# Attention into a GEGLU block: batch 0's row sums in four groups of rows, with a rewritten start

## The chip, the cores and the metric

The kernel runs on one core of one Trainium2 chip. The metric is device time in microseconds, given as the median of a few executions; the profile is of one of those executions. All times in the text that are "at" a moment count from the start of the profiled span.

## The reference

Eight batches of sliding-window attention (8 heads, 576 tokens, 64 per head, window 128, ALiBi bias) feed a gated block of 512 by 1536.

```python
scores = scale * np.matmul(q, k.transpose(0, 1, 3, 2))
mask = (rel >= 0) & (rel < window)
scores = np.where(mask, scores + bias[None], -1000000000.0)
attn = np.exp(scores - np.max(scores, axis=-1, keepdims=True))
attn = attn / (np.sum(attn, axis=-1, keepdims=True) + 1e-09)
attn_out = np.matmul(attn, v)
# ... heads side by side: x has 4608 rows (tokens) of 512
g = x @ w_gate
out = (0.5 * g * (1.0 + erf(g / sqrt(2)))) * (x @ w_val) @ w_out
```

## The kernel before

PE (the matrix engine) does everything in the order in which it is written: transposes, scores, row sums, products with the values, gate and value products, output products. Heads go in four pairs, `c`. A batch is cut into part one (320 tokens) and part two (256). Sums of the exponentials are products with a stationary operand of ones, one column group of PE for each pair, with a column for every token; DVE takes the reciprocal, and four f32 products spread it over the 64 rows of each head:

```python
def sums(b, s):
    ps = bank()
    for j, a, e in PIECES[s]:
        for i in (0, 1):
            for c in range(4):
                nc.tensor.matmul(
                    out=ps[32 * c:32 * c + 32, a:e],
                    lhsT=ones[:, min(j, 1), i, :], rhs=prob(b, s, c, i, j, e - a), ...)
    ...
    lo, hi = PART[s]
    nc.vector.reciprocal(sumrow[b][:, lo:hi], ps[:, 0:hi - lo])     # 128 x 320, then 128 x 256

def spread_pe(b, s, copies=(nc.scalar.copy, nc.vector.tensor_copy)):
    lo, hi = PART[s]
    pss = [bank() for _ in range(4)]
    for c, ps in enumerate(pss):
        nc.tensor.matmul(out=ps[:, 0:hi - lo], lhsT=sel[32 * c:32 * c + 32, ...],
                         rhs=sumrow[b][32 * c:32 * c + 32, lo:hi], ...)
    for c, ps in enumerate(pss):
        copies[c % 2](out=recip[b][:, c, lo:hi], in_=ps[:, 0:hi - lo])
```

Products of zeros stand in front of some steps. They compute nothing; each is 512 columns wide. `keep_busy(n)` puts `n` of them before the next bank that is used:

```python
def bank():
    ps = psum.tile([128, 512], FP32, name="ps")
    for _ in range(heat.pop()):
        nc.tensor.matmul(out=ps, lhsT=zeros[:, 0:128], rhs=zeros, start=True, stop=True)
    heat.append(0)
    return ps
```

The order of batch 0, which is all that the change touches, is:

```python
keep_busy(8); first((0, 1))                 # transposes of tokens 0-383; keep_busy(1) before the keys'
keep_busy(1)
scores(0, 0, (0, 1), lambda: (keep_busy(1), first((2,)), first((3,))))
scores(0, 0, (2, 3))
scores2(0)
keep_busy(2); rest((0, 1)); rest((2, 3))    # transposes of tokens 384-575
keep_busy(4); sums(0, 0)
keep_busy(2); scores(0, 1, (0, 1), None, masks)
keep_busy(3); spread_pe(0, 0)
values(0, 0, range(4))
scores(0, 1, (2, 3), None, masks)
for f in range(4): gate_val(0, f, 0, 320, tails)
...
sums(0, 1)
...
for f in (4, 5): gate_val(0, f, 0, 320)
spread_pe(0, 1)
values(0, 1, range(4))
gate_val(0, 6, 0, 320)
```

The softmax here doesn't subtract the row's maximum and nothing guards it: scores larger than these inputs give would overflow.

## Time and profile before

| what | before |
|---|---|
| time, median of 3 (range) | 359.17 us (358.96 to 359.27) |
| profiled span | 357.6 us |
| PE busy | 97% |
| keys of the first transfer landed | 7.03 us |
| first reciprocal | 15.29 to 17.45 us |
| first gate product on the value side | 21.11 us |
| first transposes of batch 1 | 40.66 us |
| end of the last copy on ACT | 354.99 us |

### The profile page before, as it was taken

Reading aid. Unit: us, or ns where it says so; the run is one execution under the profiler, and the core shown is the slowest. Engines: PE = TensorE matmul, PEld = TensorE weight load, DVE = VectorE, ACT = ScalarE, POOL = GpSimd, SP = SyncE. Lnnn points to the kernel's source line nnn. Section 1 sums busy time; section 2 is a strip of 40 time slices with the busy share of each in tenths; the row PEclk is TensorE's granted clock in tenths of the full one; section 3 lists DMA queues with packets and bytes.
Section 4 is the critical chain, followed back from the end, with each engine's and each line's share of the span. In section 5 each row is a group of like instructions: output and inputs, shape, how many; then the busy total and the mean of one; then the engine's idle time right before and its main releaser. Section 6 shows DMA issues by size and latency. Waiting matters only on the chain.

```text
span 357.6 us, 6808 instructions
## 1 busy us (share of the span) xinstructions
PE 346.0 (97%) x2703; PEld 172.8 (48%) x2746; DVE 188.9 (53%) x309; ACT 185.5 (52%) x342; POOL 105.8 (30%) x141
## 2 busy tenths in 40 slices
PE   7799999999999999999999999999999999999996
PEld 2468545444455445445454545445454444444444
DVE  4877568443888746656446554746473503302420
ACT  4874496535878367532973288336833123313322
POOL 8954579501920085002920094004000000000000
PEclk9999999999999999999999999999999999999999
DMA  9999999999999299683997599969206030011002
GB/s 104 176 193 195 200 148 181 164 179 137 151 140 140 49 188 179 120 173 68 142 199 147 110 103 211 154 132 71 86 33 132 4 116 0 3 59 59 2 20 97
DMA packets 146144, 42.61 MB, mean 119 GB/s; under 512 B 133144, under 2 KB 139032, under 8 KB 146112
## 3 DMA queue, kind: packets, MB, share of 16 engines
q0 software_dynamic: 106880, 18.88, 69.3%
q1 hardware_dynamic: 36432, 17.31, 21.7%
q10 hardware_dynamic: 2800, 5.99, 7.8%
q8 instruction: 21, 0.34, 0.4%
q14 instruction: 11, 0.09, 0.1%
HBM read 43.65 MB, written 9.53 MB: 149 GB/s over the span
## 4 chain that ended last, share of the span: by engine, by line
PE 87%; DVE 5%; ACT 4%; issue 2%; DMA 1%; POOL 0%; DVEq 0%; ACTq 0%; POOLq 0%
PE ps L310 49%; PE ps L333 24%; PE ps L291 4%; PE ps L179 4%; DVE r L254 3%; ACT P L186 2%; PE ps L245 2%; DMA ks<-in_k_dram 1%; PE ps L274 1%; DVE kT L150 1%; PE ps L140 1%; PE ps L347 1%; PE ps L70 0%; DVE hT L317 0%; DVE xT L297 0%
## 5 line engine op out<-in xcount | busy, mean ns | idle before, releaser
L317 DVE TENSOR_TENSOR hT<-ps,gelu 128x512 bf16<-128x512 f32 (+2 forms) x115 | 74.0, 653 | 106.1 <-PE ps L310 91.7
L316 ACT ACTIVATE gelu<-ps 128x512 bf16<-128x512 f32 (+2 forms) x115 | 65.2, 571 | 116.9 <-PE ps L310 112.3
L310 PE MATMUL ps<-xT,wv 128*128 128x512 bf16 (+2 forms) x453 | 111.4, 366 | 0.6
L310 PE MATMUL ps<-xT,wg 128*128 128x512 bf16 (+2 forms) x444 | 110.9, 366 | 1.0
L333 PE MATMUL ps<-wo,hT 128*128 128x512 bf16 x402 | 94.9, 380 | 0.8
L186 ACT ACTIVATE P<-ps 128x512 bf16<-128x512 f32 x144 | 73.4, 625 | 8.1 <-PE ps L179 8.1
L310 PEld LDWEIGHTS <-wv 128*128 128x128 bf16 x460 | 44.7, 98 | 49.1 <-issue 0.3
L310 PEld LDWEIGHTS <-wg 128*128 128x128 bf16 x460 | 43.2, 98 | 47.4 <-issue 0.6
L189 DVE TENSOR_TENSOR P<-P,emask 128x1024 bf16<-128x1024 bf16 x72 | 48.2, 691 | 32.0 <-ACT P L186 31.9
L333 PEld LDWEIGHTS <-hT 128*128 128x128 bf16 x420 | 38.8, 98 | 47.9 <-issue 4.0
L96 POOL DMA_DIRECT2D vb<-in_v_dram x40 | 34.0, 905 | 6.4 <-DMA ks<-in_k_dram 1.6
L338 ACT COPY osb<-ps 128x512 f32<-128x512 f32 x31 | 18.6, 601 | 29.6 <-PE ps L333 28.7
L254 DVE RECIPROCAL r<-ps 128x320 f32<-128x320 f32 (+1 forms) x16 | 30.7, 1937 | 2.9 <-PE ps L245 2.9
L525 POOL COPY mark<-hT 1x2 bf16<-1x2 bf16 x4 | 0.7, 175 | 100.3 <-DVE hT L317 100.3
L297 DVE TENSOR_TENSOR xT<-ps,rb 128x320 bf16<-128x320 f32 (+1 forms) x64 | 24.6, 445 | 7.3 <-DMA rb<-rd 5.3
L96 POOL DMA_DIRECT2D qs<-in_q_dram x30 | 25.2, 864 | 7.5 <-PE ps L179 2.9
L96 POOL DMA_DIRECT2D ks<-in_k_dram x30 | 25.4, 899 | 1.0 <-DMA qs<-in_q_dram 0.9
L179 PE MATMUL ps<-qT,kT 64*128 64x256 bf16 (+1 forms) x384 | 21.8, 244 | 2.3 <-DVE kT L150 1.8
L179 PEld LDWEIGHTS <-kT 64*128 64x128 bf16 x384 | 13.0, 94 | 14.3 <-issue 9.1
L291 PE MATMUL ps<-P,vb 128*64 128x128 bf16 (+2 forms) x384 | 18.2, 243 | 0.1
L291 PEld LDWEIGHTS <-vb 128*64 128x64 bf16 x384 | 14.7, 110 | 5.8 <-issue 5.6
L245 PEld LDWEIGHTS <-ones 128*32 128x32 bf16 x384 | 7.6, 96 | 4.9 <-issue 4.3
(51 smaller groups left out, 113.3 us busy)
## 6 DMA issues: line engine op xcount, KB each, us to landing
out_dram<-osb SPq DMA_DIRECT2D x35, 256.0 KB, 3.4
rb<-rd ACTq DMA_DIRECT2D x10, 576.0 KB, 7.6
vb<-in_v_dram POOLq DMA_DIRECT2D x32, 128.0 KB, 6.8
qs<-in_q_dram POOLq DMA_DIRECT2D x24, 128.0 KB, 5.4
ks<-in_k_dram POOLq DMA_DIRECT2D x24, 128.0 KB, 6.3
wg<-in_moe_w_gate_dram POOLq DMA_DIRECT2D x4, 384.0 KB, 8.8
wv<-in_moe_w_val_dram POOLq DMA_DIRECT2D x4, 384.0 KB, 9.9
wo<-in_moe_w_out_dram POOLq DMA_DIRECT2D x2, 768.0 KB, 16.2
```

The lines of the kernel that those rows point to most:

```text
L96: nc.gpsimd.dma_start(out=t[lo:128, j, :].rearrange("p (h d) -> p h d", h=H), in_=src[b][:, 128 * j - 64 + lo:128 * j + 64, :].rearrange(" ...
L179: nc.tensor.matmul(out=ps[:, col:col + 128 * n].rearrange("p (n t) -> p n t", n=n), lhsT=blocks(kT, b, i, c, j, 1).rearrange("p n t -> p ( ...
L186: nc.scalar.activation(out=dst, in_=src, func=AF.Exp, scale=0.125)
L189: nc.vector.tensor_tensor(out=dst, in0=dst, in1=m, op=ALU.mult)
L254: nc.vector.reciprocal(sumrow[b][:, lo:hi], ps[:, 0:hi - lo])
L291: nc.tensor.matmul(out=ps[64 * i:64 * i + 64, a:e], lhsT=vb[b % 2][:, j, 64 * h:64 * h + 64], rhs=prob(b, s, c, i, j, e - a), start=(j == ...
L297: nc.vector.tensor_tensor(out=xT[:, c, b * S + lo:b * S + hi], in0=ps[:, 0:hi - lo], in1=recip[b][:, c, lo:hi], op=ALU.mult)
L310: nc.tensor.matmul(out=ps[:, 0:hi - lo], lhsT=w[:, c, 128 * f:128 * (f + 1)], rhs=xT[:, c, t0 + lo:t0 + hi], start=(c == 0), stop=(c == 3))
L316: nc.scalar.activation(out=gl[:, 0:hi - lo], in_=pg[:, 0:hi - lo], func=AF.Gelu)
L317: nc.vector.tensor_tensor(out=hid[g][:, f, lo:hi], in0=pv[:, 0:hi - lo], in1=gl[:, 0:hi - lo], op=ALU.mult)
L333: nc.tensor.matmul(out=po, lhsT=hid[g][:, f, 128 * t:128 * (t + 1)], rhs=wo[:, f, :], start=(f == 0), stop=(f == NF - 1))
L338: (nc.vector.tensor_copy if g < 2 and t < 2 else nc.scalar.copy)(out=osb, in_=po)
```

## The change

The intent is to shorten the exposed reciprocal. The time of the reciprocal goes with its columns (2.16 us for 320, 1.76 us for 256, on 128 rows each), so the sums are laid over four groups of 32 rows with 80 columns each (part one) or 128 (part two), in place of 320 and 256 columns. This costs more and narrower products for the sums (72 for 24) and the spread (16 for 4). Around it, the tokens of batch 0 are cut otherwise (runs of 80 x 4 and 128 x 2), POOL no longer builds `sel`, the last mask is cut in two, pair 0 of part two is scored before the spread and the other three after it, one of the two covering gates goes behind the second spread, and the counts of zeros are new.

```diff
-    RUNS = ((0, 128, 3), (384, 96, 2))
+    RUNS = (((0, 80, 4), (320, 128, 2)), ((0, 128, 3), (384, 96, 2)))
...
+    WIDE = (80, 128)
+    def sums0(s):
+        w = WIDE[s]
...
+        for c, i, j, a, e in todo:
+            for x in range(a // w, (e + w - 1) // w):
+                lo, hi = max(a, w * x), min(e, w * x + w)
+                g = x if s == 0 else 2 * x + c // 2
...
+        nc.vector.reciprocal(row(0)[:, PART[s][0]:PART[s][0] + w], ps[:, 0:w])
+    def spread0(s, copies):
...
+        n = (4, 2)[s]
+        for k in range(n):
+            for g, ps in enumerate(pss):
+                nc.tensor.matmul(
+                    out=ps[:, w * k:w * k + w],
+                    lhsT=sel[32 * g:32 * g + 32, 2 * k:2 * k + 2, :].rearrange("p i m -> p (i m)"),
+                    rhs=row(0)[32 * g:32 * g + 32, lo:lo + w], start=True, stop=True,
+                    tile_position=(32 * g, 0))
...
-    for c in range(4):
-        nc.gpsimd.affine_select(
-            out=sel, in_=sel, compare_op=ALU.not_equal, fill=1.0,
-            base=-32 * c, pattern=[[-16, 2], [0, 64]], channel_multiplier=1)
...
-                keep_busy(1)
+                keep_busy(2)
...
     first((0, 1))
+    keep_busy(5)
+    scores(0, 0, (0, 1), lambda: (keep_busy(2), first((2,)), first((3,))))
     keep_busy(1)
-    scores(0, 0, (0, 1), lambda: (keep_busy(1), first((2,)), first((3,))))
     scores(0, 0, (2, 3))
     scores2(0)
-    keep_busy(2)
+    keep_busy(4)
     rest((0, 1))
     rest((2, 3))
-    keep_busy(4)
-    sums(0, 0)
+    keep_busy(3)
+    sums0(0)
     masks, tails = [], []
+    scores(0, 1, (0,), None, masks)
     keep_busy(2)
-    scores(0, 1, (0, 1), None, masks)
-    keep_busy(3)
-    spread_pe(0, 0)
+    spread0(0, (act, dve, act, dve))
     values(0, 0, range(4))
-    scores(0, 1, (2, 3), None, masks)
+    scores(0, 1, (1, 2, 3), None, masks)
```

More of the change, by code (lines that the diff above doesn't have):

```diff
@@ L82 @@
     ones = consts.tile([128, 2, 2, 32], BF16, name="ones")
+    ones4 = consts.tile([128, 2, 8 * 36], BF16, name="ones4")
+    ones8 = consts.tile([128, 4 * 36], BF16, name="ones8")
     emask = consts.tile([128, H, 256], BF16, name="emask")
-    sel = consts.tile([128, 2, 64], FP32, name="sel")
+    sel0 = consts.tile([128, 8], FP32, name="sel0")
+    sel = consts.tile([128, 8, 64], FP32, name="sel")
     mark = consts.tile([1, 2], BF16, name="mark")
@@ L102, in load_qk, with runs @@
         load(ks[b % 2], k, b)
-    RUNS = ((0, 128, 3), (384, 96, 2))
-    def runs(t, n):
-        first, parts, r = RUNS[n]
-        lo = 1536 * n
+    RUNS = (((0, 80, 4), (320, 128, 2)), ((0, 128, 3), (384, 96, 2)))
+    def runs(what, b, n):
+        first, parts, r = RUNS[b][n]
+        t, lo = (qs, ks)[what][b], 1536 * n
+        if (b, n) == (0, 1):
+            t, lo = vb[1], 512 + 1024 * what
         return t.rearrange("p j x -> p (j x)")[0:parts, lo:lo + 512 * r].rearrange(
@@ L113, in load_runs @@
     def load_runs(b, n, h0, h1):
-        first, parts, r = RUNS[n]
-        for t, src in ((qs[b], q), (ks[b], k)):
+        first, parts, r = RUNS[b][n]
+        for what, src in ((0, q), (1, k)):
             nc.gpsimd.dma_start(
-                out=runs(t, n)[:, h0:h1, :],
+                out=runs(what, b, n)[:, h0:h1, :],
                 in_=src[b][h0:h1, first:first + parts * r, :].rearrange(
@@ L134, in transpose_runs @@
     def transpose_runs(b, n, what, c, ps):
-        first, parts, r = RUNS[n]
-        src = runs((qs, ks)[what][b], n)
+        first, parts, r = RUNS[b][n]
+        src = runs(what, b, n)
         for x in range(r):
@@ L145, in untangle @@
     def untangle(copy, b, n, what, c, ps):
-        first, parts, r = RUNS[n]
+        first, parts, r = RUNS[b][n]
         dst = by_pair((qT, kT)[what][b])[:, c, 64 + first:64 + first + parts * r]
@@ L200, in scores2 @@
             exp(P[:, :, i, :], ps[i].rearrange("p (c n) -> p c n", c=4))
-        args = (P.rearrange("p c i n -> p (c i) n"), emask[:, :, 0:128])
         if later is None:
-            mask(*args)
+            for i in (0, 1):
+                mask(P[:, :, i, :], emask[:, i:8:2, 0:128])
         else:
-            later.append(args)
+            later.append((P.rearrange("p c i n -> p (c i) n"), emask[:, :, 0:128]))
     def scores(b, s, cs, then=None, later=None):
@@ L237, with row @@
     sumrow, recip = {}, {}
+    def row(b):
+        if b not in sumrow:
+            sumrow[b] = r_pool.tile([128, S], FP32, name="r")
+            recip[b] = r_pool.tile([128, 4, S], FP32, name="rb")
+        return sumrow[b]
+    WIDE = (80, 128)
+    def sums0(s):
+        w = WIDE[s]
+        ps = bank()
+        todo = []
+        for c in range(4):
+            for i in (0, 1):
+                for j, a, e in ((0, 0, 192), (1, 64, 320)) if s == 0 else PIECES[1]:
+                    todo.append((c, i, j, a, e))
+        if s == 0:
+            todo += [(c, i, 2, 192, 320) for i in (0, 1) for c in range(4)]
+        mms = []
+        for c, i, j, a, e in todo:
+            for x in range(a // w, (e + w - 1) // w):
+                lo, hi = max(a, w * x), min(e, w * x + w)
+                g = x if s == 0 else 2 * x + c // 2
+                h = 2 * c + i
+                mms.append((g, ones4[:, min(j, 1), 32 * h:32 * h + 32] if s == 0 else
+                            ones8[:, 32 * (h % 4):32 * (h % 4) + 32],
+                            prob(0, s, c, i, j, e - a)[:, lo - a:hi - a], lo - w * x, hi - w * x))
+        for n, (g, lhsT, rhs, lo, hi) in enumerate(mms):
+            nc.tensor.matmul(
+                out=ps[32 * g:32 * g + 32, lo:hi], lhsT=lhsT, rhs=rhs,
+                start=all(m[0] != g for m in mms[:n]), stop=all(m[0] != g for m in mms[n + 1:]),
+                skip_group_check=True)
+        nc.vector.reciprocal(row(0)[:, PART[s][0]:PART[s][0] + w], ps[:, 0:w])
+    def spread0(s, copies):
+        lo, hi = PART[s]
+        w = WIDE[s]
+        pss = [bank() for _ in range(4)]
+        n = (4, 2)[s]
+        for k in range(n):
+            for g, ps in enumerate(pss):
+                nc.tensor.matmul(
+                    out=ps[:, w * k:w * k + w],
+                    lhsT=sel[32 * g:32 * g + 32, 2 * k:2 * k + 2, :].rearrange("p i m -> p (i m)"),
+                    rhs=row(0)[32 * g:32 * g + 32, lo:lo + w], start=True, stop=True,
+                    tile_position=(32 * g, 0))
+        for g, ps in enumerate(pss):
+            c, x = ((0, g), (2 * (g % 2), g // 2))[s]
+            copies[g](out=recip[0][:, c:c + n, lo + w * x:lo + w * x + w],
+                      in_=ps[:, 0:n * w].rearrange("p (c x) -> p c x", c=n))
     def sums(b, s):
@@ L249, in sums @@
                         skip_group_check=True)
-        if b not in sumrow:
-            sumrow[b] = r_pool.tile([128, S], FP32, name="r")
-            recip[b] = r_pool.tile([128, 4, S], FP32, name="rb")
         lo, hi = PART[s]
-        nc.vector.reciprocal(sumrow[b][:, lo:hi], ps[:, 0:hi - lo])
+        nc.vector.reciprocal(row(b)[:, lo:hi], ps[:, 0:hi - lo])
     flat = {}
@@ L275, in spread_pe @@
                 out=ps[:, 0:hi - lo],
-                lhsT=sel[32 * c:32 * c + 32, :, :].rearrange("p i m -> p (i m)"),
+                lhsT=sel[32 * c:32 * c + 32, 0:2, :].rearrange("p i m -> p (i m)"),
                 rhs=sumrow[b][32 * c:32 * c + 32, lo:hi], start=True, stop=True,
@@ L361 @@
         nc.vector.memset(by_pair(t)[:, :, 0:64], 0.0)
-    nc.vector.memset(sel, 0.0)
     nc.gpsimd.affine_select(
@@ L365 @@
         base=0, pattern=[[-1, 128]], channel_multiplier=1)
+    nc.vector.tensor_reduce(
+        out=sel0, in_=ident.rearrange("p (g h r) -> p h g r", g=4, r=4)[:, :, :, 0],
+        op=ALU.add, axis=mybir.AxisListType.X)
+    nc.vector.tensor_copy(out=sel, in_=sel0.unsqueeze(2).to_broadcast((128, 8, 64)))
     load_runs(0, 0, 4, 8)
@@ L375 @@
     load_runs(0, 1, 0, 8)
-    step = DFF // 4
     load_v(0, (0, 1, 2))
-    load_w(0, step)
-    for c in range(4):
-        nc.gpsimd.affine_select(
-            out=sel, in_=sel, compare_op=ALU.not_equal, fill=1.0,
-            base=-32 * c, pattern=[[-16, 2], [0, 64]], channel_multiplier=1)
-    load_w(step, 2 * step)
+    load_w(0, 256)
+    load_w(256, 640)
     load_v(0, (3, 4))
-    for n in (2, 3):
-        load_w(step * n, step * (n + 1))
+    load_w(640, 1024)
+    load_w(1024, DFF)
     for n in (0, 1):
         load_runs(1, n, 0, 8)
-    nc.vector.memset(ones, 0.0)
-    for i in range(2):
-        nc.vector.memset(ones[64:128, 0, i, 16 * i:16 * i + 16], 1.0)
-        nc.vector.memset(ones[:, 1, i, 16 * i:16 * i + 16], 1.0)
+    for t in (ones, ones4, ones8):
+        nc.vector.memset(t, 0.0)
+    by4 = ones4.rearrange("p n (h x) -> p n h x", x=36)
+    nc.vector.memset(by4[64:128, 0, :, 0:4], 1.0)
+    nc.vector.memset(by4[:, 1, :, 0:4], 1.0)
+    for lo in (0, 16):
+        nc.vector.memset(ones8.rearrange("p (h x) -> p h x", x=36)[:, :, lo:lo + 4], 1.0)
+    for i, lo, hi in ((0, 0, 4), (1, 4, 8), (0, 8, 16), (1, 16, 32)):
+        nc.vector.memset(ones[64:128, 0, i, lo:hi], 1.0)
+        nc.vector.memset(ones[:, 1, i, lo:hi], 1.0)
     for i in range(2):
@@ L416, in rest @@
             for k, c in enumerate(cs):
-                transpose_runs(0, 1, w, c, ps[:, 192 * k:192 * k + 192])
+                transpose_runs(0, 1, w, c, ps[:, 256 * k:256 * k + 256])
             untangle(act, 0, 1, w, slice(cs[0], cs[-1] + 1), ps)
@@ L444 @@
         tail()
-    sums(0, 1)
+    sums0(1)
     for tail in tails[2:4]:
         tail()
-    for f in (4, 5):
-        gate_val(0, f, 0, 320)
-    spread_pe(0, 1)
+    gate_val(0, 4, 0, 320)
+    spread0(1, (act, dve, act, dve))
     values(0, 1, range(4))
+    gate_val(0, 5, 0, 320)
     gate_val(0, 6, 0, 320)
```

## The prediction

> **What bounds the kernel now.** I read the page first, then busy time by stretches of 5 us, then the chain of work up to 60 us, and last the timelines of PE, DVE and ACT over the first 31 us.
>
> ```profile
> PE 346.0 (97%) x2703; PEld 172.8 (48%) x2746; DVE 188.9 (53%) x309; ACT 185.5 (52%) x342; POOL 105.8 (30%) x141
> 0.00:5.00 5.00, 3.60 (x8) 1.04 (x8) 1.95 (x14) 1.28 (x1) 3.89 (x10) 1.00 0.54 56
> 5.00:10.00 5.00, 3.93 (x59) 2.19 (x59) 2.42 (x5) 4.05 (x12) 4.89 (x9) 1.00 1.56 167
> 10.00:15.00 5.00, 3.67 (x75) 2.12 (x78) 4.90 (x9) 4.45 (x11) 4.79 (x8) 1.00 1.77 164
> 15.00:20.00 5.00, 4.34 (x72) 2.46 (x68) 3.71 (x5) 3.62 (x9) 4.77 (x7) 1.00 1.30 198
> 20.00:25.00 5.00, 4.80 (x34) 3.04 (x32) 4.22 (x9) 4.76 (x9) 2.69 (x4) 1.00 1.70 190
> ```
>
> The columns of a stretch are its length, then PE, PEld, DVE, ACT and POOL busy (instructions), granted clock, DMA share and GB/s. PE is busy 97% of the span, and what it lacks lies mostly before 20 us; part of its work there is products of zeros that only keep it warm. From 21 us on PE has little else to wait for. So the change, which rewrites batch 0's first 31 us, can be worth only what moves the moment at which PE starts its unbroken run of gate products, less whatever PE work it adds after that. The chain shows that moment:
>
> ```profile
> 2.14 4.89 DMA ks<-in_k_dram
> ...
> 7.47 1.03 DVE kT L150 x2
> ...
> 14.55 0.72 PE ps L245 x24
> 15.27 0.02 issue
> 15.29 2.17 DVE r L254
> 17.46 0.14 issue
> 17.60 0.87 PE ps L274 x8
> ...
> 20.98 4.10 PE ps L310 x29
> 25.08 0.56 PE ps L245 x24
> 25.63 2.28 PE ps L310 x16
> 27.91 0.64 PE ps L274 x8
> ```
>
> Columns: start, time, what. The reader is to see one DVE instruction, the reciprocal of the row sums (L254, 128x320), holding everything for 2.17 us between the sums (L245) and the products that spread them (L274), and the second half's sums and spread lying inside a run of PE work, where their reciprocal is covered. The timelines give unit costs:
>
> ```profile
> 15.29 2.16 DVE L254 RECIPROCAL r<-ps 128x320 f32<-128x320 f32 x1 [0.40 <-PE ps L245]
> 25.69 1.76 DVE L254 RECIPROCAL r<-ps 128x256 f32<-128x256 f32 x1 [1.06 <-PE ps L245]
> 13.52 1.04 PE L70 MATMUL ps<-zeros 128*128 128x512 bf16 x4
> 11.26 2.46 POOL L380 TENSOR_SCALAR_AFFINE_SELECT sel<-sel 128x128 f32<-128x128 f32 x4
> ```
>
> **What the Trainium skill says.** The page "VectorE: DVE Perf Modes", section "Walkthrough: the 8-slice pipeline in each mode", says the reciprocal is an iterative divide repeated on the pipe, so it costs several cycles an element. The trace agrees: the two lengths differ by 64 columns and 0.40 us, 6.3 ns a column and 0.15 us fixed. "TensorE: Matmul & The Clock Gate", section "Back-to-back issue gap", says a product of few columns still pays a floor of some 25 ns. In the trace, products in the four column groups start under 4 ns apart and one group's next product waits only for its own columns (55 ns at 128); nothing there is narrower than 96 columns, so the floor is untested. The same page, section "LDWEIGHTS (loading the stationary operand)", gives columns over 1.2 GHz, 107 ns for 128; the trace has 109 ns between an f32 weight load and the next in the same row group. "SBUF — State Buffer", section "SBUF: two separate sides", says that DVE instructions with two SBUF inputs and GpSimd instructions that read SBUF block each other. The trace agrees: the masks of 128x1024 took 0.77 us beside POOL's affine selects of sel and 0.68 us elsewhere.
>
> **The change part by part.**
>
> Reciprocals. Four groups of rows make the first 80 columns wide: 80 x 6.3 ns + 0.15 = 0.65 us instead of 2.16, **1.5 us off the chain**. The second is 128 wide: 0.95 instead of 1.76, but that one is hidden today.
>
> Sums, first half. 9 pieces a head, 72 products for 24. In order, with only the same column group waiting, they take about 0.85 us by my count of columns (x=1, 2, 3 carry 160 columns a head, then 8 pieces of the second tile use two groups alone), against 0.6 now. They need the masks one after the other, not all at once, so the last mask holds back only the tail of 16 products. What starts them, though, is PE itself. Before the sums PE has: scores of pair 3 (0.55, starting near 11.5), 4 zero products (0.1 + 4 x 0.217 from the line with four of them), 32 transposes of 128 columns in pairs (16 x 0.056 = 0.89, was 0.68 for 96 columns), 3 zeros (0.75) and some 0.1 for each change of tiling. That puts the first sum at 14.85, the last at 15.7, the reciprocal at 15.95 to 16.6. Now it ends at 17.45: **0.85 us earlier**, not 1.5. The masks, freed of POOL and with the last one cut in two, would be done near 14.6.
>
> Start. The first runs carry 160 KB instead of 192, so keys that land at 7.03 (the trace gives the landing of each transfer) should land near 6.5. DVE's preparation grows: it waits for ident from POOL (3.29), reduces, fills sel (128x512 f32, 0.35 to 0.6), sets ones4 and ones8 and a dozen small pieces at 0.06 to 0.12 each; I get 6.2 to 6.5 for its end where it is 3.0 now, so the first copies, at 5.57 now, slip. Copies of 320 columns save 0.07 each over the 0.465 from copy to copy now. Key copies end near 8.0; the five zeros, 1.2 us from about 7.0, end near 8.2. The scores of the first pairs are then where they are today, 8.1 to 8.9; I count **nothing gained** up to the exponentials of pair 2 (11.13 today).
>
> Spread, first half. 16 products for 4, two f32 passes each. A pass of 80 columns at two cycles each takes 67 ns, under the 109 ns of its weight load, so weights set the pace: 8 x 109 + 0.08 = 0.95 us for 0.75, and the copies start some **0.25 us later** behind the spread's first product. Copies and the four products with the values are as many and as wide as now, so they keep their length. Gates: 20.98 - 0.85 + 0.25 = 20.4, **0.6 us earlier**.
>
> Second half, where PE has no slack. Sums: 32 products; groups 2x + c/2 leave only two column groups at work for each c, about 0.95 us for 0.56: **+0.4**. Spread: 4 passes at 109 ns, 0.5 for 0.64: -0.1. Gate 4 alone (1.1 us) stands over the 0.95 us reciprocal and its semaphores, where two gates stood over 1.76: +0.1 of waiting. Scores of three pairs after the values give ACT six exponentials (3.0 us) before the Gelu table; they end near 22.0, as the four do now (21.95), so Gelu is not later.
>
> Weights. In the trace loads land in the order of issue at about 190 KB/us. The second wv lands at 23.05 and is first used near 24.4. The first wg and wv become 256 columns, 128 KB less each, which at that rate brings the first wv in 1.3 us earlier (19.14 now) and the next pair also; every one stays about 1 us ahead of its use. The selects that POOL no longer does (2.46 us) free issue slots only, and the queue is backlogged.
>
> Sum: -0.6 + 0.4 - 0.1 + 0.1 = -0.2 us, 359.0. The zero counts look fitted to waits seen on the chip, which says the author found PE idle where I see it busy; that pulls me to **358.7 us**.
>
> **Rivals.** *PE stays ahead.* If transposes and zeros end before the masks, the whole 1.5 us of the reciprocal counts; with -1.5 + 0.25 + 0.4 the time is 358.2 or a little less with an earlier start. For it: earlier keys, smaller copies. Against it: PE's own list above is 14.85 without a single wait. *The narrow products are dear.* If 80-column pieces run at the pace of their weight loads, some 55 ns a group instead of 36, the first sums take 1.3 us, and with DVE's longer preparation delaying the first copies the gain is gone and the added PE work shows: 359.3 to 359.7. For it: PEld entries of L245 take 96 ns each; against: 128-column pieces already run at 55 ns with no sign of it. *A transfer or table takes the place.* Gates 0.6 us earlier could wait for the weights of block 2; the landing times leave 1 us, so this would cost under 0.5 us: 359.2.
>
> **Range and chances.** The three give 358.2 to 359.7; an unseen gain at the start widens it below: 357.8 to 359.5 for 8 in 10. Two per cent are 7.2 us, more than all PE idle time in the five stretches above (4.7 us), so within 2% has 0.98, faster 0.01, slower 0.01.
>
> **What would show it.** Right: reciprocals of 0.65 and 0.95 us; the first one ending near 16.6; first sums starting near 14.85 with no wait before them; the spread lasting about 1 us; gates unbroken from 20.4; second sums near 0.95 us; from 31 us on the same work at a shift of a few tenths. Wrong: sums that start when the last mask ends (first rival), sums of over 1.2 us (second), a wait of L310 for wg or wv (third), or a first score after 8.6, which would mean that the preparation on DVE sits on the path.

## The result

| | before | after |
|---|---|---|
| time, median of 4 (range) | 359.16 us (358.96 to 359.27) | 359.10 us (358.81 to 359.46) |
| profiled span | 357.6 us | 357.4 us |
| first reciprocal | 15.29 to 17.45 | 15.43 to 16.09 |
| first value-side gate product | 21.11 | 20.29 |
| first transposes of batch 1 | 40.66 | 39.96 |
| end of the last copy on ACT | 354.99 | 354.30 |
| span behind that copy | 2.64 | 3.09 |

The ratio is 0.9999, with a 95% interval of 0.9982 to 1.0017: the same. Ratios here are the mean time of one kernel's fast runs over the mean of the other's fast runs of the same rounds, so they are not quite the ratio of the medians that are quoted. The time is inside the predicted range, 0.4 us above the 358.7 that was named.

First the totals and busy time by stretches of 5 us, in the kernel after (columns as in the prediction):

```profile
PE 347.6 (97%) x2811; PEld 174.8 (49%) x2855; DVE 188.7 (53%) x327; ACT 186.0 (52%) x342; POOL 103.5 (29%) x137
...
5.00:10.00 5.00, 4.85 (x81) 2.37 (x76) 3.05 (x14) 4.18 (x12) 5.00 (x8) 1.00 1.32 144
10.00:15.00 5.00, 4.31 (x116) 2.54 (x118) 4.29 (x9) 4.67 (x10) 5.00 (x7) 1.00 1.93 173
15.00:20.00 5.00, 4.65 (x115) 3.44 (x103) 3.14 (x7) 3.80 (x9) 2.69 (x5) 1.00 1.42 198
```

From 5 to 20 us PE is busy 13.8 us where it was 11.9, and yet its real work is done less than 1 us sooner: the difference is mostly zeros. By the source there are 17 of them between the first transposes and the first sum, where there were 9, and eight more at 0.22 us each are 1.8 us. Next, the chain of work of the kernel after (start, time, what):

```profile
6.84 1.19 PE ps L70 x5
8.03 0.54 PE ps L186 x8
...
13.75 0.75 PE ps L70 x3
14.51 0.90 PE ps L278 x31
15.41 0.02 issue
15.43 0.67 DVE r L282
16.10 0.09 issue
16.19 1.21 PE ps L292 x32
17.40 0.88 DVE rb L299 x2
...
19.75 4.51 PE ps L370 x32
24.26 0.80 PE ps L278 x32
```

L70 is the zeros, L186 scores, L278 sums, L282 the reciprocal, L292 the spread, L370 gates. In the place of the transfer of keys that headed this chain before, PE's own zeros stand ahead of the first scores and of the first sums. Keys landed at 5.95, 1.1 us sooner than before; two zeros issued after the query transposes held the key transposes until 6.36, and five more held the scores until 7.96, 0.13 us before their old time of 8.09. The masks ended at 14.29 (14.90 before), but the first sum came at 14.44 (14.48): PE was not waiting for masks, it was working through transposes and zeros. The reciprocals, from the DVE timeline of the kernel after, are what was aimed at:

```profile
15.43 0.66 DVE L282 RECIPROCAL r<-ps 128x80 f32<-128x80 f32 x1 [1.14 <-PE ps L278]
25.11 0.96 DVE L282 RECIPROCAL r<-ps 128x128 f32<-128x128 f32 x1 [0.60 <-PE ps L278]
```

1.50 us came off the first one. At the gates 0.82 us of it is left, at the first transposes of batch 1 0.70 us. The timelines show the last of these, before and then after, with the start in the first column:

```profile
40.66 0.45 PE L140 MATMUL ps<-ident,qs 128*64 128x128 bf16 x10
```

```profile
39.96 0.45 PE L147 MATMUL ps<-ident,qs 128*64 128x128 bf16 x10
```

The same 0.70 us is there 314 us later, at the last copy on ACT, again before and then after:

```profile
354.62 0.37 ACT L351 COPY osb<-ps 128x256 f32<-128x256 f32 x1 [0.94 <-PE ps L347]
```

```profile
353.92 0.37 ACT L411 COPY osb<-ps 128x256 f32<-128x256 f32 x1 [0.94 <-PE ps L407]
```

So the change did make the work 0.70 us shorter. The span became only 0.24 us shorter, since behind the last copy there are now 3.09 us in the place of 2.64. Two questions are left: what happens behind the last copy, and why the new zeros, which seem to eat the gain at the start, are there at all.

### The profile page after: what moved, and what is told of

Same layout as the page of the kernel before. It is cut to its first block, busy times and chain, and to the rows that moved or that the text cites. A ratio compares the mean times of both kernels' runs of the same rounds, so it can differ in the third digit from the quotient of the medians.

```text
span 357.4 us, 7028 instructions
## 1 busy us (share of the span) xinstructions
PE 347.6 (97%) x2811; PEld 174.8 (49%) x2855; DVE 188.7 (53%) x327; ACT 186.0 (52%) x342; POOL 103.5 (29%) x137
## 4 chain that ended last, share of the span: by engine, by line
PE 89%; DVE 4%; ACT 4%; issue 2%; DVEq 0%; ACTq 0%
PE ps L370 50%; PE ps L393 23%; PE ps L351 5%; PE ps L186 4%; ACT P L193 2%; DVE r L314 2%; PE ps L70 2%; PE ps L308 2%; PE ps L147 1%; PE ps L334 1%; PE ps L407 1%; DVE kT L157 1%; PE ps L292 1%; PE ps L278 0%; DVE hT L377 0%
## 5 line engine op out<-in xcount | busy, mean ns | idle before, releaser
L370 PE MATMUL ps<-xT,wv 128*128 128x512 bf16 (+2 forms) x453 | 111.4, 366 | 0.6
L370 PE MATMUL ps<-xT,wg 128*128 128x512 bf16 (+2 forms) x444 | 110.4, 366 | 0.8
L370 PEld LDWEIGHTS <-wv 128*128 128x128 bf16 x460 | 44.7, 98 | 48.8
L370 PEld LDWEIGHTS <-wg 128*128 128x128 bf16 x460 | 43.2, 98 | 47.1 <-issue 0.3
L196 DVE TENSOR_TENSOR P<-P,emask 128x1024 bf16<-128x1024 bf16 (+1 forms) x79 | 49.0, 641 | 30.7 <-ACT P L193 30.2
L314 DVE RECIPROCAL r<-ps 128x320 f32<-128x320 f32 (+1 forms) x14 | 26.8, 1936 | 1.4 <-PE ps L308 1.4
L186 PE MATMUL ps<-qT,kT 64*128 64x256 bf16 (+1 forms) x384 | 21.9, 244 | 1.6 <-DVE kT L157 1.1
L186 PEld LDWEIGHTS <-kT 64*128 64x128 bf16 x384 | 13.2, 94 | 13.6 <-issue 10.0
L70 PE MATMUL ps<-zeros 128*128 128x512 bf16 x24 | 8.8, 485 | 1.3 <-DVE zeros L418 1.2
```

Source lines behind the costliest of these rows:

```text
L186: nc.tensor.matmul(out=ps[:, col:col + 128 * n].rearrange("p (n t) -> p n t", n=n), lhsT=blocks(kT, b, i, c, j, 1).rearrange("p n t -> p ( ...
L196: nc.vector.tensor_tensor(out=dst, in0=dst, in1=m, op=ALU.mult)
L314: nc.vector.reciprocal(row(b)[:, lo:hi], ps[:, 0:hi - lo])
L370: nc.tensor.matmul(out=ps[:, 0:hi - lo], lhsT=w[:, c, 128 * f:128 * (f + 1)], rhs=xT[:, c, t0 + lo:t0 + hi], start=(c == 0), stop=(c == 3))
```

## The experiments

Each is an edit of the kernel after. "Shift" is the moment of the same DVE instructions (the products into hT, from the second part of group 0 to the last group) against the kernel before, so -0.70 for the change itself. The zero counts are written in the order of the source: before the key transposes, before the first scores, before the transposes of pairs 2 and 3, before the scores of pairs 2 and 3, before `rest`, before the sums, before the spread. The change has 2, 5, 2, 1, 4, 3, 2.

### again: the changed kernel, unchanged

There is no edit. It shows how far runs of one kernel differ.

> The changed kernel once more. In the two profiles every instruction from 31 us to the last copy stands 0.70 us earlier than before the change, yet the spans differ by 0.2 us, because the end behind the last copy took 3.14 us instead of 2.64. Theory T1 (the 0.7 us is real, the longer end belongs to this program): the shift is again 0.7 us, the end again 3.1 us, and the ratio is near 0.9995. T2 (the long end was chance): the end is near 2.65 us and the ratio near 0.998. T3 (nothing is gained, the shift itself varies from run to run by that much): the shift at 31 us differs from 0.7 by over 0.3.

359.42 us (359.17 to 359.80, 6 runs) against 359.38 for the kernel before in the same job (358.78 to 360.94, 11 runs): ratio 0.9998, interval 0.9981 to 1.0016. The shift is -0.54, 3.10 us behind the last copy (where the expectation has 3.14 for the kernel after, its trace has 3.09). The kernels are the same in time, and a few tenths of shift come and go with the landing of the keys: 6.48 us here, 5.95 in the trace of the kernel after.

### pool_pad: nine tiny instructions on POOL

```diff
+        if g == 7:
+            for _ in range(9):
+                nc.gpsimd.memset(mark, 0.0)
         if g == 0:
             for t in (qs[1], ks[1]):
```

The change had taken four selects, with their waits, from POOL's list. This puts instructions back on POOL late in the kernel, where they wait for nothing and nothing waits for them.

> Nine tiny POOL memsets, late in the program when POOL is idle, so that POOL has as many instructions as before the change; they touch nothing on the chain. T1a (the long end comes from where the last POOL instructions fall in the stream of instructions): the end behind the last copy falls from 3.1 to 2.65 us and the time falls by 0.4 to 0.5 us against the plain changed kernel. If the end stays at 3.1 it has nothing to do with POOL's count; if both kernels show 2.65 it was chance.

358.79 us (358.31 to 359.33) against 359.38 for before and 359.42 for again in the same job; ratio 0.9981, interval 0.9962 to 1.0001. The shift is -0.69 and the last copy starts at 353.93, as in the kernel after (353.92), but behind the copy there are 2.65 us in place of 3.09. The count of instruction transfers by queue, on the page of the kernel after and then on that of pool_pad (queue, kind, packets, MB, share), differs by one:

```profile
q14 instruction: 10, 0.08, 0.1%
```

```profile
q14 instruction: 11, 0.09, 0.1%
```

The page of before has 11 too. Their times in the trace show which one: before and pool_pad have an 8 KB transfer on this queue at 245 us, in the middle of the work; after and again have none there, but one at 357.7 us, just behind the end of the profiled span. What is shown is that instructions added to POOL, which do no work, take back 0.44 us. Over all runs the end goes with the padding without exception: 3.08 to 3.10 us in the four traces of kernels without it that have the change (after, again, old_sums, old_zeros), 2.64 or 2.65 in before and in all padded kernels. How the late transfer and the longer end hang together was not shown: it starts only after the span has ended, and the trace does not say which engine it serves.

### old_sums: the new start with the old sums and spread

```diff
-    sums0(0)
+    sums(0, 0)
-    spread0(0, (act, dve, act, dve))
+    spread_pe(0, 0)
```

The same was done for part two; zeros, runs and order stay as changed.

> The changed kernel with the old sums, reciprocals and spread for batch 0; all else of the change stays. Theory: the reciprocal goes back to 2.16 us on the chain (+1.5), the first sums shrink by 0.3, the first spread by 0.35, and the second half gives back 0.25 of sums; the gates start 0.8 to 1.1 us later than in the changed kernel and from 31 us on the shift against the kernel before is between 0 and -0.1 us, time +0.5 to +0.7 us (ratio to before near 1.000). Rival (the start of the change, not the sums, gave the 0.7): shift at 31 us stays near -0.7.

360.43 us, ratio 1.0024 (1.0006 to 1.0041). The shift is +0.79. The fair comparison is with again, whose keys landed as late (6.48 us for 6.53): from +0.79 to -0.54 the four groups of rows are worth 1.3 us in this frame, more than I expected. The medians of the same job differ by 1.0 us. The first reciprocal is exposed as before. The second is exposed too, since only one gate covers it now. From the PE timeline of old_sums:

```profile
26.21 0.71 PE L370 MATMUL ps<-xT,wv 128*128 128x320 bf16 x4
27.68 0.71 PE L334 MATMUL ps<-r,sel 32*128 32x256 f32 x8 [0.76 <-DVE r L314]
```

Its reciprocal takes 1.76 us from 25.78, and PE waits 0.76 us for it between the gate and the spread. The new sums and the new order belong together; the frame (zeros, runs, order) alone is a loss of 0.6 to 0.8 us, the less with keys that land early.

### old_zeros, few_zeros and no_zeros: what the zeros do

```diff
-  2, 5, 2, 1, 4, 3, 2      # as changed
+  1, 1, 1, 0, 2, 4, 3      # old_zeros: the counts of before
+  1, 2, 0, 0, 1, 0, 0      # few_zeros, with the padding on POOL
+  0, 0, 0, 0, 0, 0, 0      # no_zeros, with the padding on POOL
```

The eight zeros at the very start stay in all three. The two zeros that the kernel before has ahead of the scores of part two have no place in the new order and are not in old_zeros.

> The changed kernel with the zero products counted as before the change (1, 1, 1, 0, 2, 4, 2, 3 in place of 2, 5, 2, 1, 4, 3, 0, 2). Theory that PE's own zeros hold the chain (sums started at 14.44 with no wait, masks were done at 14.28): keys' transposes start near 6.0 instead of 6.36, the first scores 0.3 to 0.4 earlier, the sums at 13.6 to 14.0, and the shift at 31 us grows from -0.7 to between -0.9 and -1.2. Rival (DVE's preparation and masks hold it): the sums start no earlier than 14.2 and the shift stays within 0.1 of -0.7. Rival (fewer zeros let PE's clock fall): products of 512 columns take twice 0.217 us somewhere between 6 and 20 us and the shift is lost.

359.77 us, ratio 1.0012 (0.9992 to 1.0032), shift -0.10.

> The changed kernel with the POOL memsets of pool_pad and few zero products: 8 at the start as before, then 1, 2, 0, 0, 1, 0, 0, 0 in place of 2, 5, 2, 1, 4, 3, 0, 2. Theory (zeros on PE hold the chain): first scores at 7.4 instead of 7.96, the exponentials of pair 2 near 10.0 instead of 10.8, first sums by 13.2 and the first reciprocal by 14.2 instead of 15.43. In old_zeros such an earlier reciprocal was lost again to 0.91 us in which PE, in the middle of the spread, waited for nothing that the profile shows, behind a 16 KB load of instructions that started at 14.5 instead of 12.5. If that stop belongs to an instruction supply that can't keep up, it shows again between the sums and the values, and the shift at 31 us against before stays above -1.0; if it was chance, the shift is near -1.5, and from there the weights (second wv landing at 21.2) are next to wait for. Rival: fewer zeros let PE's clock fall, 128x512 products near 0.43 us apart before 20 us.

359.69 us, ratio 0.9988 (0.9955 to 1.0021), shift +0.32.

> As few_zeros but with no zero product at all after the first 8. Theory that PE needs no more warming, since no idle stretch is longer than about 1.5 us: as few_zeros within 0.2 us. Rival that the zeros earn their place: keys' transposes and scores run at half pace (80-column pairs 67 ns apart instead of 36, 256-column pairs 0.21 us apart instead of 0.107), and the sums start at least 0.5 us later than in few_zeros.

359.26 us, ratio 0.9985 (0.9952 to 1.0019), shift +0.90 in the profiled run.

Without most zeros the first sum indeed comes early: 12.83 us in few_zeros for 14.44, the reciprocal is done at 14.48 for 16.09. And then the gain is lost in two ways, both named in the expectation. From the PE timeline of few_zeros, and its stretch from 15 to 20 us:

```profile
14.53 0.67 PE L292 MATMUL ps<-r,sel 32*128 32x80 f32 x13 [0.23 <-DVE r L282]
16.46 1.38 PE L292 MATMUL ps<-r,sel 32*128 32x80 f32 x19 [1.25 <-issue]
```

```profile
15.00:20.00 5.00, 3.75 (x52) 3.07 (x51) 2.33 (x6) 1.58 (x4) 2.55 (x5) 0.67 1.41 198
```

PE stopped in the middle of the spread for 1.25 us, and what ended the stop was nothing that the profile shows ("issue"). After it the granted clock was halved for 3.41 us (16.70 to 20.11): 0.67 on average in the stretch. The halved clock is not in every run: by the mean granted clock that each run lists (0.995 or less) it was in 5 of 6 runs of few_zeros, 3 of 6 of no_zeros and 4 of 6 of few_and_four, but also in 3 of the 11 runs of before in the first job. So part of what these kernels lose differs from run to run. old_zeros stops in the same products:

```profile
16.99 1.12 PE L292 MATMUL ps<-r,sel 32*128 32x80 f32 x27 [0.91 <-issue]
```

no_zeros stopped 1.11 us and few_and_four (below) 1.16 us. The place is not tied to a product of the spread: 5, 13, 17 and 13 of them came before the stop in old_zeros, few_zeros, no_zeros and few_and_four. It is tied to a count: sorted by start, the first instruction after the stop is the 450th PE or PEld record of the trace in all four (two records of the sequencer at the very start are counted). Each time a transfer of 16 KB on the other instruction queue (q8) had landed 1.2 to 1.5 us earlier:

| | 16 KB starts | lands | record 450 starts | stop |
|---|---|---|---|---|
| old_zeros | 14.50 | 15.46 | 16.99 | 0.91 |
| few_zeros | 13.98 | 14.93 | 16.46 | 1.25 |
| no_zeros | 14.82 | 15.78 | 17.25 | 1.11 |
| few_and_four | 14.52 | 15.50 | 16.72 | 1.16 |
| after | 12.50 | 13.48 | 16.19 | none |
| before | 15.20 | 16.10 | 22.88 | none |

The trace of the kernel after lacks some 40 records; in again, the same kernel, record 450 starts at 15.82, also without a stop. The trace does not say which engine the queue serves. But its count of loads goes with PE's records: 21 in the traces of 5449 and 5534 PE and PEld instructions, 22 in those of 5631 to 5792, 23 in those of 5808 and 5822.

That zeros also do what they are meant for is seen between few_zeros and no_zeros: the exponentials of pair 2 began at 9.85 and 10.45 us, though the key transposes of no_zeros had begun sooner (5.78 for 6.03). Here the rival of the expectation came true in the profiled run: the scores of 256 columns stood 0.21 us apart, the 12 products of pairs 2 and 3 took 1.04 us for 0.62, and the first sum came 0.6 us later (13.43 for 12.83). The medians do not show this loss (359.26 for 359.69), and the profiled run was the slowest of the six.

The theory that follows from the stops is that PE runs out of loaded instructions. A zero product takes PE some 0.22 us for two records, many times as long as a narrow sum, so wide zeros slow the use of instructions and hide a late load. It is tested below.

### four_groups: the second sums in an order that uses all four column groups

```diff
-        for c in range(4):
-            for i in (0, 1): ...            # c = 0, 1 use groups 0 and 2; c = 2, 3 use groups 1 and 3
+            todo += [(c + d, i, j, a, e) for c in (0, 1) for i in (0, 1)
+                     for j, a, e in ((2, 0, 128), (3, 0, 256), (4, 128, 256)) for d in (0, 2)]
```

With the padding on POOL, and the zeros as changed.

> pool_pad with the 32 products of the second sums in another order, so that pairs c and c+2 alternate and all four column groups work. Theory: these sums took 0.80 us instead of 0.56 because only two groups were at work; they fall to 0.50, everything behind them moves by 0.3 minus what the gate between sums and reciprocal can't cover (up to 0.1): shift at 31 us -0.9 to -1.0 instead of -0.70, time 0.2 to 0.3 us under pool_pad. Rival (the number of products is the cost): they stay at 0.75 or more.

358.68 us, ratio 0.9967 (0.9931 to 1.0003). The PE timelines, of the kernel after and then of four_groups, with the next gate as the mark of the end of the sums:

```profile
24.19 0.87 PE L278 MATMUL ps<-P,ones 128*32 128x128 bf16 x32
24.99 0.72 PE L370 MATMUL ps<-xT,wg 128*128 128x320 bf16 x4
```

```profile
24.36 0.64 PE L280 MATMUL ps<-P,ones 128*32 128x128 bf16 x32
24.93 0.72 PE L372 MATMUL ps<-xT,wg 128*128 128x320 bf16 x4
```

From the first sum to the next gate it is 0.80 us as changed and 0.57 us in the new order, with 32 products in both. So the cost of the second sums is not their number but that two column groups stood idle; the shift is -0.75 although all before the sums ran 0.17 us later than in after (the keys were no later, 5.80 us for 5.95, but their transposes took 0.64 us for 0.48). That is short of the -0.9 to -1.0 that was expected. In time this is 0.1 us below pool_pad, of another job, which no timing here separates.

### few_and_four: few zeros and the new order together

The edits of few_zeros and of four_groups, with the padding.

> few_zeros and four_groups together, the version that should beat both kernels if the parts add: shift at 31 us that of few_zeros less another 0.2 to 0.3 us. If PE's zeros can go and nothing else steps in: 358.0 us or a little less; if the instruction supply steps in: 358.5 to 358.8.

359.29 us, ratio 0.9979 (0.9945 to 1.0012), shift +0.33. The reciprocal is done at 14.83, then PE stops 1.16 us, and the clock is halved from 17.98 to 21.39. The two gains do not add: the stop comes first.

### few_early: the same, with the eight starting zeros made narrow and many

```diff
-        for _ in range(heat.pop()):
-            nc.tensor.matmul(out=ps, lhsT=zeros[:, 0:128], rhs=zeros, start=True, stop=True)
+        n = heat.pop()
+        w = 64 if n == 64 else 512
+        for _ in range(n):
+            nc.tensor.matmul(out=ps[:, 0:w], lhsT=zeros[:, 0:128], rhs=zeros[:, 0:w],
+                             start=True, stop=True)
...
-    keep_busy(8)
+    keep_busy(64)
```

If PE stops because a load of instructions comes late, then 112 more records in the first 5 us, where PE has time, must make the load start early, and the stop must go. If the stop belongs to the spread, nothing changes.

> few_and_four, with the 8 first zero products of 512 columns replaced by 64 of 64 columns: the same time on PE while it waits for the first queries (64 x 53 ns at the half clock is 3.4 us, as 8 x 0.43), but 112 PE instructions more. In old_zeros, few_zeros, no_zeros and few_and_four PE stood still for 0.9 to 1.25 us after its 449th recorded instruction, whatever that was, about 1.5 us after a 16 KB load of instructions had landed. If instruction supply is the cause, the 449th instruction now lies in the first sums and its load starts some 3 us earlier: no stop in the spread, no half clock, the spread near 14.6 runs through in 1.1 us, values from 15.7, gates from about 18.7, then perhaps a wait for the second wv (21.1): shift at 31 us between -1.0 and -2.0, time 357.3 to 358.2. If the stop belongs to the spread itself (reciprocal, banks, the clock), it stays in the spread and the time stays near 359.

357.58 us (357.35 to 358.98) against 359.19 for before in the same job (358.43 to 360.05): ratio 0.9958, interval 0.9939 to 0.9976. The first 16 KB load starts at 7.82 and lands at 8.76; record 450 runs at 13.35. From the PE timeline and its stretch:

```profile
14.74 1.13 PE L297 MATMUL ps<-r,sel 32*128 32x80 f32 x32 [0.42 <-DVE r L287]
```

```profile
15.00:20.00 5.00, 4.79 (x87) 3.69 (x84) 3.93 (x9) 4.24 (x10) 2.69 (x5) 1.00 1.40 199
```

All 32 passes of the spread run through, the only wait before them is for the reciprocal, and the clock stays at 1.00. The first value-side gate comes at 18.84, and the shift is -1.73: 2.1 us from few_and_four in the profiled runs, by an edit of the starting zeros alone. Up to 0.2 us of this is the landing of the second keys (12.19 for 12.35). By the medians, each against the kernel before in its own job, it is 1.5 us. The zeros behind the start are as few as in few_and_four, and yet none of the six runs has a mean clock under 0.998: few zeros alone do not halve it. Now a transfer does come into view. The waits of PE's weight loads show it:

```profile
PEld L375 <- DMA wv<-in_moe_w_val_dram: 1.0, 2, 0.6
```

On PE itself the products behind these two waits start 0.21 and 0.42 us late. This version beats both kernels: the interval against before lies wholly below 1, and again had put before and after at the same time.

### short_start and old_zeros_early: the narrow starting zeros with more zeros behind

```diff
-    keep_busy(8)
+    keep_busy(64)             # both; 64 columns each, as in few_early
   # short_start: 2, 5, 2, 1, 4, 3, 2 and the new order of four_groups
   # old_zeros_early: 1, 1, 1, 0, 2, 4, 3 and the old order of the second sums
```

Both have the padding.

> Control: four_groups with only the 64 short products at the start. It has no stop in the spread, so both theories say the same as four_groups within 0.2 us (shift near -0.75 to -0.95); a difference beyond that would mean that the short products do something else, to the clock for one.

359.99 us, ratio 1.0021 (1.0000 to 1.0041), shift +0.71. Narrow starting zeros are no gain in themselves. The expectation (near -0.75) missed by 1.46 us. About 0.5 of it is the landing of the first keys, 6.83 us where four_groups had 5.80: the sums began 0.53 us later. The rest is mostly a stop. The spread ran without a stop, but another one came later, from the PE timeline of short_start:

```profile
21.10 0.34 PE L189 MATMUL ps<-qT,kT 64*128 64x128 bf16 x4 [0.83 <-issue]
```

This is record 706 of PE, 256 after record 450, and a 16 KB load had landed at 19.66, 1.44 us earlier. 16 KB in 256 instructions are 64 bytes each. That is the second support of the theory: a stop in other work, in other products, at the next multiple of what one load brings.

> old_zeros with the POOL memsets and the 64 short products at the start. Instruction supply: the 0.91 us stop in the spread goes, the first spread near 15.6 runs through, and the shift at 31 us is near -1.2 instead of -0.1. Otherwise it stays near -0.1.

358.95 us, ratio 0.9994 (0.9972 to 1.0016), shift +0.22. The stop in the spread is gone, as in few_early. But the shift missed what I had expected: the second part's keys landed late in this run, at about 13.0 us where few_early had 12.19, and PE waited 1.02 us for them before the transposes of `rest`. Record 706 also starts 0.5 us after the record before it, 1.53 us after a load. The old counts of zeros then stand on the path behind this. So the removal of the stop is confirmed, and what the old counts would be worth on a run with early keys stays open.

### small_loads: smaller weight loads against the waits of few_early

```diff
-    load_w(256, 640)
+    load_w(256, 512)
+    load_w(512, 640)
     load_v(0, (3, 4))
-    load_w(640, 1024)
-    load_w(1024, DFF)
+    load_w(640, 896)
+    load_w(896, 1280)
+    load_w(1280, DFF)
```

> few_early with the weights in six loads of 256, 256, 128, 256, 384 and 256 columns instead of four of 256, 384, 384 and 512. In few_early PE stood for 0.21 us at block 2 and 0.42 us at block 5 until a wv had landed (21.17 and 27.35). Theory that weights are the next bound there: those two land 1.3 us earlier each (19.9 and 26.0), both waits go, the shift at 40 us grows by 0.5 to 0.6 us over few_early's and the time is near 357.0. Rival (more loads, more POOL work and later landings behind them): a new wait of the gate products at blocks 7 to 10 or at batch 1's keys takes it back, within 0.2 us of few_early.

358.51 us, from 357.39 to 361.88, against 360.54 for before, which itself ran from 358.89 to 362.62 on this chip: ratio 0.9925 (0.9884 to 0.9966). The profiled run was the slowest of the six: its keys landed late (9.12 and 13.75) and its clock was halved from 12.05 to 22.29. PE was some 4 us late at the gates, so that it did not wait for the weights there proves nothing. Its two best times, 357.39 and 357.65, are those of few_early. Three of its six runs have a mean clock of 0.995 or less, with the same few zeros as few_early, which had none: that late keys and few zeros together do this is likely, but not tested. The run is inconclusive.

## Why the prediction was right, and where it was not

The sum in the prediction was -0.2 us; the result is the same to within the runs. That the sum came so close is luck: two misses cancel. The work became 0.70 us shorter, where I had 0.2, and the end became 0.45 us longer, of which I knew nothing. What was right in kind is the mechanism at the start.

**The reciprocals** were right: 0.66 and 0.96 us, for 0.65 and 0.95.

**The first sums** were right in kind, off in size. 72 products took 0.90 us for the 0.85 that I had counted, and the start was PE's own list of work, as argued: 14.44 us with no wait recorded, for 14.85. The mis-sized term is "nothing gained" at the start: the exponentials of pair 2 began at 10.78 us, where I left them at 11.13. The reciprocal thus ended 1.36 us earlier than before, not 0.85.

**The spread and what follows it.** I had 0.95 us and a loss of 0.25. The spread took 1.06 us, at 112 ns from pass to pass where I had 109. The copies began 1.07 us earlier, so 0.34 of the spread's lead of 1.41 was lost there. The multiplications began only 0.85 us earlier: each copy now holds a quarter of the tokens of all four pairs, so the first multiplication needs all four copies where it used to need one. I had missed this dependence; it cost 0.2 us. At the gates 0.82 us were left, for 0.6.

**The second half.** The sums cost 0.24 us more, not 0.4, and four_groups shows the reason that I gave, two idle column groups: with all four at work they cost 0.57. The spread of 16 passes took 0.65 us, as long as the old one (0.64), so the -0.1 was wrong. The wait behind gate 4 was about 0.1 us, as predicted. The shift at 30 us is -0.59. Another 0.11 comes in the next gate, the first of 192 columns: before, its fourth product started 0.19 us after the third, where the others are 0.08 apart, just after the last multiplication had ended at 30.96; in the kernel after the multiplications are done at 29.19, since two gates now stand behind them, and there is no wait.

**The end** is the step that was missing altogether. I took it that a shift at 31 us is a shift of the time. pool_pad shows that it is not: a few instructions on POOL, of no use, decide over 0.44 us at the end.

**The pull to 358.7** rested on the zero counts being "fitted to waits seen on the chip". PE does stand idle with the old counts (0.91 us in old_zeros), so that reading fits. But I took it for a gain that I did not see. It was a loss that the new zeros hide: a stop for instructions that the narrow products bring forward, and a halved clock after it.

**The rivals.** "PE stays ahead" did not come true in the changed kernel, as its own zeros keep PE from being early; few_early, which removes them without the stop, gets there and below (357.58 for the 358.2 of that rival, which by its own sum of -0.85 is 358.3). "The narrow products are dear" falls with the 0.90 us. "A transfer takes the place" did not happen at -0.70. At -1.73 it did, with the two waits of 0.63 us together.

**What stays open:** why the 16 KB loads start when they do (in few_zeros 0.5 us before the reciprocal is done, in few_early 6 us earlier), what takes another 1.2 to 1.5 us from landing to the next instruction, and by what means the instructions on POOL lengthen the end.

## What to carry to other kernels

When a shorter dependency moves the time less than its own length, follow one late milestone through both traces: here it showed that the gain was there at the last copy and was lost only behind it. Here many narrow products outran the supply of instructions; an "issue" stop at the same count of instructions in several kernels was its mark here, and it went when more small instructions were issued earlier, where the engine had nothing to do. Products of zeros that were fitted on the chip may hide such a stop, so take them away and look at the trace before counting them as waste.

## What the Trainium skill lacked or had wrong

- Supply of instructions. "Trainium Architecture — The Big Picture", section "The software stack", has 64-byte instructions that are brought into each engine's memory when the program is loaded. "Runtime: NRT & Kernel Launch", section "Instruction fetch mechanics", adds that an engine goes on fetching them while it runs, in blocks of 16 KiB or 256 instructions, and calls the cost of crossing a block "mostly hidden". The sizes agree (stops at records 450 and 706, 256 apart; 22 loads of 16 KB on one queue in the kernel after). The cost was not hidden here: stops of 0.83 to 1.25 us in five kernels, when a load landed only 1.2 to 1.5 us before its first instruction ran. What no page has is this time between landing and first instruction.
- "TensorE: Matmul & The Clock Gate", section "What's actually happening": the clock falls after an idle window of about 3.4 us. The length of the cold stretch agrees (3.41 us in few_zeros, no_zeros and few_and_four), but the half clock was granted after stops of only 1.1 to 1.25 us among other short gaps, which that rule does not cover, while in old_zeros, with 0.91 us, the mean clock of the run stayed at 0.999. The floor of some 25 ns for a narrow product, which the prediction took from the same page, holds at most within one column group: with four groups in use, 72 products of 16 to 80 columns took 0.90 us, 12.5 ns each. This is no contradiction, since the page's section "Measured speedup vs the span model" counts only about 4 ns for each further product in another tile of the array.
- The end of a program: no page has that it depends on instructions of POOL. The span behind the last copy was 2.64 to 2.65 or 3.08 to 3.10 us, and instructions of POOL that did no work made the difference.
